# First sequence's scores from unsplit float32 queries and keys, the second's from two parts each

## The chip, the cores and the metric

The kernel runs on one core of one Trainium2 chip. A core has TensorE (PE; its weight loads are listed apart as PEld), VectorE (DVE), ScalarE (ACT), GpSimd (POOL) and SyncE (SP), which each work through a queue of instructions in order and wait for each other by semaphores, and DMA engines that move data between the chip's memory and the on-chip SBUF. TensorE writes to PSUM, eight banks of 512 float32 columns. The metric is the device time of one execution in microseconds, the median of several runs.

## The reference

Three layers follow each other: attention with a sliding window of 128 and 4 sink tokens, a gated MLP, and a layer of 8 experts of which each token takes at most one.

```python
def _attn_ref(q, k, v, n_sink, window):          # q, k, v: (2, 8, 768, 64)
    scores = scale * np.matmul(q, k.transpose(0, 1, 3, 2))
    ...
    scores = np.where(is_sink | in_window, scores, -1000000000.0)
    a = softmax(scores)
    return np.matmul(a, v)

x = attn_out as 1536 tokens of 512
x = (silu(x @ w_gate) * (x @ w_val)) @ w_out     # 512 -> 1536 -> 512
# experts: tokens with x @ w_skip > 0 add gate * relu(x @ w1[e]) @ w2[e], e = argmax(x @ w_gate)
```

## The kernel before, in words

The 1536 tokens are twelve tiles of 128: tiles 0 to 5 are the first sequence, 6 to 11 the second. Attention goes through 48 steps j, one for each tile n and each of four pairs of heads. Step A (step_a) transposes a tile's queries and keys of one pair on TensorE into a PSUM bank (tqk), ScalarE copies the bank to SBUF as the type F32R (fp32r in the rows), a rounded float32, and VectorE subtracts that from the bank, so that a second tile holds what the rounding left. These are kq0x and kq1x for pair x, the first and the second part; each has the keys of the current and of the last tile, four sink keys and the queries. At a sequence's first tile GpSimd copies the sink keys to their place. Step B (step_b) makes the scores of both heads (s0, s1) with three products each: first part by first part, and first by second both ways; the heads lie in partitions 0 to 63 and 64 to 127 of the tiles. VectorE adds the mask and reduces (line 282), ScalarE takes exponentials, VectorE and ScalarE scale the probabilities p. Step D transposes p, and step E multiplies with the values (vb, float32) and writes a tile of the MLP's input, xt, again in two parts.

PSUM is divided by use: two banks "acc", two "acq", two "gv", and two "att". Scores take acc for tiles 0 and 1, acq for tiles 2 and 3, and from tile 4 on att, where the transposes tqk, tpt, tsk and the product with the values (xps) also live. A bank is given out again when its last reader is done, and tqk has two readers, ScalarE's copy and VectorE's subtraction.

The MLP runs in six phases over groups of tiles and 12 chunks of 128 hidden columns. Its weights arrive as pairs of 32-bit words and are converted (lines 135 to 138: two steps on ScalarE, two on VectorE), then split into two parts in a ring of buffers (ScalarE copies, GpSimd or VectorE subtracts). ScalarE's tanh (line 491) evacuates the gate's product of a chunk, in all 52 times. While attention makes the first two tiles, each of its steps adds two small matmuls (warm) that keep TensorE at work. The main program writes attention steps between MLP steps by a fixed quota; a scheduler then sets the order of each engine's queue. From the second MLP phase on, attention of later tiles fills in between MLP matmuls; at the end come the experts.

The helpers that the rows name by line: 69 is act_copy (ScalarE), 72 is lo_of (the subtraction).

## Time and profile before

| | |
|---|---|
| runs | 648.02, 646.52, 643.59 us; median 646.52 |
| profiled execution | 643.09 us, its span from first to last instruction 641.4 us |
| TensorE busy | 593.4 us, 93% of the span |
| VectorE busy | 459.6 us, 72% |
| ScalarE busy | 397.2 us, 62% |
| GpSimd busy | 197.7 us, 31% |
| mean granted TensorE clock | 0.969 of 2.4 GHz |

The profile shows one execution. Busy shares of the whole span are averages over an attention and weight stage, an MLP stage and an expert stage, which have different limits, so views by stretch say more. Ends of matmuls are modelled; their starts are the surer number.

### The profile page before, as it was taken

To read this page: it belongs to the slowest core of one execution; us is meant where nothing else is said; L and a number is where in the kernel's file an instruction comes from. 1 tells how busy PE (TensorE), PEld (TensorE's weight loads), DVE (VectorE), ACT (ScalarE), POOL (GpSimd) and SP (SyncE) were. 2 spreads that over 40 slices of the span, in tenths; PEclk is the share of its full clock that TensorE was granted. 3 is DMA by queue.
4 is the path that set the end of the run, shared out by engine and by line. 5 is a ranking of instruction groups with operands and counts; after the bars stand their busy time and mean duration, and the time that the engine had idled before them with its cause. 6 is when DMAs were issued, how large, how long until landed. Compare 5 with 4: busy or idle time off the path is not lost. (4 is left out here: it accounts for less than half of the span.)

```text
span 641.4 us, 10897 instructions
## 1 busy us (share of the span) xinstructions
PE 593.4 (93%) x3489; PEld 478.6 (75%) x3489; DVE 459.6 (72%) x1163; ACT 397.2 (62%) x892; POOL 197.7 (31%) x289
## 2 busy tenths in 40 slices
PE   4979889889999999999999999999998999999993
PEld 2657667757677787777778899989986777777762
DVE  5789888787656557665665467768848698879961
ACT  4899998899555436554554456657535774856730
POOL 4355657263423022110202030011105353537411
PEclk8798999797999999999999999999999999999998
DMA  8576775464301030200001500003205876977901
GB/s 205 135 196 181 199 204 176 145 193 132 65 2 35 16 106 11 50 1 18 1 1 35 211 30 1 1 35 109 66 34 158 301 264 204 332 232 261 340 4 38
DMA packets 78422, 75.84 MB, mean 118 GB/s; under 512 B 43138, under 2 KB 55426, under 8 KB 78352
## 3 DMA queue, kind: packets, MB, share of 16 engines
q1 hardware_dynamic: 75840, 69.32, 35.2%
q0 software_dynamic: 2512, 5.68, 2.6%
q8 instruction: 32, 0.52, 0.3%
q14 instruction: 38, 0.31, 0.1%
HBM read 65.37 MB, written 11.98 MB: 121 GB/s over the span
## 5 line engine op out<-in xcount | busy, mean ns | idle before, releaser
L454 PE MATMUL gv<-xt,ring 128*128 128x256 f32 (+1 forms) x1248 | 234.4, 336 | 4.2 <-ACT xt L69 2.6
L454 PEld LDWEIGHTS gv<-xt,ring 128*128 128x128 f32 x1248 | 186.0, 192 | 28.6 <-ACT xt L69 3.1
L69 ACT ACTIVATE ring<-w 128x512 fp32r<-128x512 f32 x156 | 98.1, 630 | 96.0 <-PE gv L454 75.0
L72 DVE TENSOR_TENSOR ring<-w,ring 128x512 fp32r<-128x512 f32 x116 | 80.0, 691 | 47.4 <-ACT ring L69 46.8
L466 PE MATMUL acc<-ring,hh 128*128 128x512 f32 x288 | 93.7, 406 | 0.0
L72 DVE TENSOR_TENSOR w<-stage,w 128x512 fp32r<-128x512 f32 x96 | 87.7, 945 | 6.9 <-ACT w L69 4.5
L69 ACT ACTIVATE w<-stage 128x512 fp32r<-128x512 f32 x128 | 73.1, 626 | 10.6 <-DMA stage<-in_moe_w_dram 7.6
L72 POOL TENSOR_TENSOR ring<-w,ring 128x512 fp32r<-128x512 f32 x40 | 53.1, 1331 | 58.8 <-ACT ring L69 53.8
L72 POOL TENSOR_TENSOR w<-stage,w 128x512 fp32r<-128x512 f32 x32 | 46.9, 1468 | 46.8 <-ACT w L69 20.9
L316 POOL TENSOR_SCALAR_AFFINE_SELECT pt<-pt 128x256 f32<-128x256 f32 x40 | 21.0, 525 | 128.9 <-ACT pt L69 128.9
L466 PEld LDWEIGHTS acc<-ring,hh 128*128 128x128 f32 x288 | 51.3, 190 | 10.7 <-ACT hh L69 0.6
L466 PE MATMUL acc<-ring,hl 128*128 128x512 f32 x144 | 58.6, 408 | 0.0
L285 ACT ACTIVATE p<-p,st 128x132 f32<-128x132 f32 x96 | 38.2, 400 | 26.2 <-DVE st L282 26.0
L135 ACT ACTIVATE st<-st 128x512 uint16<-128x512 uint16 x36 | 49.0, 1360 | 3.9 <-DMA st<-in_moe_w_gate_dram 3.3
L869 PE MATMUL yps<-w,hT 128*128 128x512 f32 x192 | 47.1, 399 | 1.0 <-DVE w L72 0.6
L843 PE MATMUL hps<-w,xh 128*128 128x512 f32 x128 | 42.5, 412 | 0.7 <-PEq L917 0.4
L869 PEld LDWEIGHTS yps<-w,hT 128*128 128x128 f32 x192 | 35.3, 188 | 10.4 <-ACTq L917 1.0
L495 DVE TENSOR_TENSOR th<-th,gv 128x256 f32<-128x256 f32 (+1 forms) x52 | 27.1, 521 | 18.5 <-PE gv L454 16.7
L272 PE MATMUL s<-kq 64*128 64x260 f32 (+1 forms) x96 | 27.5, 388 | 11.7 <-DVE st L282 3.2
L640 POOL DMA_INDIRECT xs<-x,pi x12 | 13.3, 1104 | 81.2 <-ACT ring L69 48.6
L272 PEld LDWEIGHTS s<-kq 64*128 64x128 f32 x96 | 13.9, 192 | 31.0 <-issue 14.0
L69 ACT ACTIVATE hh<-th 128x256 fp32r<-128x256 f32 (+1 forms) x52 | 26.2, 503 | 16.6 <-DVE th L495 16.2
(171 smaller groups left out, 989.0 us busy)
## 6 DMA issues: line engine op xcount, KB each, us to landing
stage<-in_moe_w_dram SPq DMA_DIRECT2D x128, 256.0 KB, 4.5
st<-in_moe_w_gate_dram SPq DMA_DIRECT2D x12, 512.0 KB, 4.4
st<-in_moe_w_val_dram SPq DMA_DIRECT2D x12, 512.0 KB, 3.9
st<-in_moe_w_out_dram SPq DMA_DIRECT2D x12, 512.0 KB, 4.6
xs<-trash SPq DMA_DIRECT2D x8, 387.0 KB, 4.8
qk<-in_k_dram SPq DMA_DIRECT2D x12, 256.0 KB, 3.2
qk<-in_q_dram SPq DMA_DIRECT2D x12, 256.0 KB, 4.0
vb<-in_v_dram SPq DMA_DIRECT2D x12, 256.0 KB, 2.8
```

The costliest lines, as they stand in the source:

```text
L69: nc.scalar.activation(out=out, in_=in_, func=ACTF.Copy, scale=scale)
L72: (eng or nc.vector).tensor_tensor(out=out, in0=in_, in1=hi.bitcast(F32), op=ALU.subtract)
L135: nc.scalar.activation(out=h16[x + (0,)], in_=h16[x + (1,)], func=ACTF.Copy, scale=2.0 ** -13, bias=2.0 ** -14 - 0.5)
L272: m_ = nc.tensor.matmul(out=ss[h][:, 0:nk], lhsT=kq[a, pr][r, KW:PW], rhs=kq[c, pr][r, 0:nk], start=m == 0, stop=m == 2)
L285: nc.scalar.activation(out=p[:, h], in_=p[:, h], func=ACTF.Exp, scale=-1.0, bias=st[:, h:h + 1], accum_out=st[:, 2 + h:3 + h])
L316: nc.gpsimd.affine_select(out=d[:, 0], in_=d[:, 1], compare_op=ALU.is_ge, fill=0.0, base=0, pattern=[[0, 2], [1, P]], channel_multiplier=-1)
L454: nc.tensor.matmul(out=ps, lhsT=w_[:, kk * P:(kk + 1) * P], rhs=x_[:, kk, t0 * P:t1 * P], start=kk == 0 and m == 0, stop=kk == KD - 1 and ...
L466: nc.tensor.matmul(out=acc[g, t], lhsT=h_[:, s], rhs=w_, start=c == 0 and m == 0, stop=c == NFC - 1 and m == 2)
L495: nc.vector.tensor_tensor(out=th, in0=th, in1=vp, op=ALU.mult)
L640: d = nc.gpsimd.indirect_dma_start(out=xs[:, :], out_offset=bass.IndirectOffsetOnAxis(ap=pi[:, t], axis=0), in_=x2s[t], in_offset=None, bo ...
L843: nc.tensor.matmul(out=ps[half], lhsT=x_[:, kk, :], rhs=w_[:, kk, :], start=kk == 0 and m == 0, stop=kk == KD - 1 and m == 2)
L869: nc.tensor.matmul(out=y, lhsT=h_[:, c, :], rhs=w_[:, c % 4, :], start=c == 0 and m == 0, stop=c == NF2 - 1 and m == 2)
```

## The change

For tiles 0 to 5 the second parts are not made. Step A copies queries and keys to one float32 tile for each pair, and step B multiplies these as float32, one product for each head in place of three. For tiles 6 to 11 the code does what it did, with new tiles under the same tags.

```diff
--- before.py
+++ after.py
@@ -218,7 +218,12 @@
         return rest
 
 
-    kq = {(hl, pr): att.tile([P, PW], F32R, name=f"kq{hl}{pr}") for hl in range(2) for pr in range(NPAIR)}
+    kq = {}
+
+    def new_kq(pr, parts):
+        for hl in range(len(parts)):
+            kq[hl, pr] = att.tile([P, PW], parts[hl], tag=f"kq{hl}{pr}", name=f"kq{hl}{pr}")
+
     vsk = [None] * B
     prob, psk, pt, xt, skt = {}, {}, {}, {}, {}
 
@@ -242,21 +247,30 @@
         a = t[:, o:o + P]
         return bass.AP(a.tensor, a.offset, [a.ap[0], [step, 2], [1, P]])
 
+    def whole(n):
+
+        return n < NBLK
+
     def step_a(j):
 
         n, pr = divmod(j, NPAIR)
         i = n % NBLK
+        if i == 0 and n <= NBLK:
+            new_kq(pr, [F32] if whole(n) else [F32R, F32R])
         t = attp.tile([P, 512], F32, tag="att", name="tqk")
         for a, src in enumerate((kb[n], qb[n])):
             nc.tensor.transpose(out=t[:, a * P:(a + 1) * P], in_=src[:, 2 * pr:2 * pr + 2, :].rearrange("p h d -> p (h d)"), identity=ident)
         o = (i % 2) * W
         src = t[:, 0:2 * P].rearrange("p (a f) -> p a f", a=2)
-        hi, lo = (two(kq[hl, pr], o, KW - o) for hl in range(2))
-        act_copy(hi, src)
-        lo_of(lo, src, hi)
+        if whole(n):
+            act_copy(two(kq[0, pr], o, KW - o), src)
+        else:
+            hi, lo = (two(kq[hl, pr], o, KW - o) for hl in range(2))
+            act_copy(hi, src)
+            lo_of(lo, src, hi)
         if i == 0:
-            for hl in range(2):
-                nc.gpsimd.tensor_copy(kq[hl, pr][:, P:W], kq[hl, pr].bitcast(F32)[:, 0:4])
+            for hl in range(1 if whole(n) else 2):
+                nc.gpsimd.tensor_copy(kq[hl, pr][:, P:W], (kq[hl, pr] if whole(n) else kq[hl, pr].bitcast(F32))[:, 0:4])
 
     def step_b(j):
 
@@ -266,10 +280,12 @@
         odd = i % 2
         pool, tag = (accp, "acc") if n < GB else (acqp, "acq") if n < GS else (attp, "att")
         ss = [pool.tile([P, 512], F32, tag=tag, name=f"s{h}") for h in range(2)]
-        for m, (a, c) in enumerate(((0, 0), (0, 1), (1, 0))):
+        terms = ((0, 0),) if whole(n) else ((0, 0), (0, 1), (1, 0))
+        for m, (a, c) in enumerate(terms):
             for h in range(2):
                 r = slice(64 * h, 64 * h + 64)
-                m_ = nc.tensor.matmul(out=ss[h][:, 0:nk], lhsT=kq[a, pr][r, KW:PW], rhs=kq[c, pr][r, 0:nk], start=m == 0, stop=m == 2)
+                x_, y_ = kq[a, pr][r, KW:PW], kq[c, pr][r, 0:nk]
+                m_ = nc.tensor.matmul(out=ss[h][:, 0:nk], lhsT=x_, rhs=y_, start=m == 0, stop=m == len(terms) - 1)
         pe_last[:] = [m_.ins]
         if i:
```

The scheduler gives each engine a new order up to the end of the first sequence; behind it the queues are the same but for neighbours that change places. In the new file the lines from 250 on are numbered higher: 272 is 288, 282 is 298, 285 is 301, 454 is 470.

VectorE at the start, before: tmp, kt and mask are pieces of the masks, st and w are weights in conversion, kq_121 and kq_122 the second parts of the first two pairs.

```order
L72 TENSOR_TENSOR kq_121<-tqk,kq_117 128x2x128
L72 TENSOR_TENSOR kq_122<-tqk,kq_118 128x2x128
L137 TENSOR_SCALAR st<-st 128x512
L196 TENSOR_SCALAR mask_110<-kt 128x4
L213 TENSOR_TENSOR tmp<-tmp 128x128
L138 SCALAR_TENSOR_TENSOR w_96<-w_96,st 128x4x128
L196 TENSOR_SCALAR mask_110<-tmp 128x128
L137 TENSOR_SCALAR st<-st 128x512
L550 COPY seen<-first 128x9
L282 ISA p,st<-s_211,mask_109 128x132
```

The same place in the changed kernel:

```order
L196 TENSOR_SCALAR mask_110<-kt 128x4
L566 COPY seen<-first 128x9
L213 TENSOR_TENSOR tmp<-tmp 128x128
L196 TENSOR_SCALAR mask_110<-tmp 128x128
L137 TENSOR_SCALAR st<-st 128x512
L138 SCALAR_TENSOR_TENSOR w_96<-w_96,st 128x4x128
L298 ISA p,st<-s_201,mask_109 128x132
```

The two subtractions are gone, and the second weight's line 137 stands behind the first score reduction (line 298) instead of ahead of it.

ScalarE at the start, before, from its first exponential on; kq_117 and so on are the first parts, pt the transposed probabilities, st a weight in conversion.

```order
L285 ACTIVATE p,st<-p,st 128x132 x2
L69 ACTIVATE kq_119<-tqk 128x2x128
L69 ACTIVATE p<-p,st 128x132
L69 ACTIVATE kq_120<-tqk 128x2x128
L69 ACTIVATE kq_117<-tqk 128x256
L285 ACTIVATE p,st<-p,st 128x132 x2
L69 ACTIVATE pt<-tpt 128x256
L135 ACTIVATE st<-st 128x512
L69 ACTIVATE p<-p,st 128x132
```

The same place in the changed kernel:

```order
L301 ACTIVATE p,st<-p,st 128x132 x2
L69 ACTIVATE kq_220<-tqk 128x2x128
L301 ACTIVATE p,st<-p,st 128x132 x2
L69 ACTIVATE p<-p,st 128x132
L69 ACTIVATE kq_252<-tqk 128x2x128
L301 ACTIVATE p,st<-p,st 128x132
L69 ACTIVATE p<-p,st 128x132
L69 ACTIVATE pt<-tpt 128x256
L301 ACTIVATE p,st<-p,st 128x132
L69 ACTIVATE pt<-tpt 128x256
L69 ACTIVATE kq_158<-tqk 128x256
L69 ACTIVATE p<-p,st 128x132
```

The third weight's line 135 no longer stands among the attention steps of the first tiles; it follows as row 27 where it was row 16.

TensorE at tile 5, pair 1, before: gv is a gate or value product of the MLP, s0 and s1 the scores of the two heads.

```order
L454 MATMUL gv_1575<-xt1_483,ring_106 128x256
L454 MATMUL gv_1575<-xt0_482,ring_106 128x256
L272 MATMUL s0_1590<-kq01_118 128x260
L272 MATMUL s1_1591<-kq01_118 128x260
L272 MATMUL s0_1590<-kq11_122,kq01_118 128x260
L272 MATMUL s1_1591<-kq11_122,kq01_118 128x260
L272 MATMUL s0_1590<-kq01_118,kq11_122 128x260
L272 MATMUL s1_1591<-kq01_118,kq11_122 128x260
L454 MATMUL gv_1611<-xt0_482,ring_106 128x256
```

The same place in the changed kernel:

```order
L470 MATMUL gv_1460<-xt1_444,ring_106 128x256
L470 MATMUL gv_1460<-xt0_443,ring_106 128x256
L288 MATMUL s0_1475<-kq01_164 128x260
L288 MATMUL s1_1476<-kq01_164 128x260
L470 MATMUL gv_1492<-xt0_443,ring_106 128x256
```

Six score matmuls between the same MLP products have become two, which read one tile only.

## Rows read from the trace of the kernel before

**Rows 1.** Busy time by stretch: PE, PEld, DVE, ACT, POOL, granted clock, DMA share, GB/s.
```profile
0.00:30.00 30.00, 21.11 (x110) 14.28 (x112) 18.74 (x99) 19.10 (x52) 10.04 (x38) 0.77 0.69 177
30.00:106.00 76.00, 64.57 (x488) 50.96 (x484) 67.37 (x217) 70.27 (x175) 46.94 (x59) 0.98 0.69 196
106.00:165.00 59.00, 51.72 (x283) 40.55 (x282) 49.92 (x116) 51.87 (x104) 28.73 (x38) 0.88 0.49 148
165.00:480.00 315.00, 314.12 (x1940) 262.98 (x1940) 201.93 (x551) 164.80 (x388) 46.54 (x100) 1.00 0.13 40
```

**Rows 2.** ScalarE's groups up to 106 us: busy us, mean ns, idle before and releaser.
```profile
L135 ACT ACTIVATE st<-st 128x512 uint16<-128x512 uint16 x20 | 27.2, 1359 | 3.3 <-DMA st<-in_moe_w_gate_dram 3.3
L285 ACT ACTIVATE p<-p,st 128x132 f32<-128x132 f32 x40 | 15.7, 397 | 1.6 <-DVE st L282 1.5
L69 ACT ACTIVATE ring<-w 128x512 fp32r<-128x512 f32 x23 | 14.5, 629 | 1.8 <-PE gv L454 1.7
L136 ACT ACTIVATE w<-st 128x512 f32<-128x512 f32 x20 | 13.7, 684 | 0.0
L69 ACT ACTIVATE kq<-tqk 128x256 fp32r<-128x256 f32 x22 | 8.4, 382 | 3.6 <-PE tqk L251 3.5
L69 ACT ACTIVATE p<-p,st 128x132 f32<-128x132 f32 x20 | 8.0, 398 | 1.6 <-DVE st L287 1.4
```

**Rows 3.** Timeline of ScalarE at the first and the seventh tanh: start, us.
```profile
52.16 0.38 ACT L491 ACTIVATE th<-gv 128x256 f32<-128x256 f32 x1 [1.07 <-PE gv L454]
...
106.02 0.39 ACT L491 ACTIVATE th<-gv 128x256 f32<-128x256 f32 x1
```

**Rows 4.** TensorE's waits from 30 to 165 us: total us, times, longest.
```profile
PE tpt L309 <- DVE st L282: 3.2, 3, 1.8
PE s L272 <- DVE kq L72: 2.8, 2, 2.5
```

**Rows 5.** Tile kq up to 139 us: duration ns min/median/max, first and last start.
```profile
L272 PE MATMUL s<-kq,kq x96: 274/280/584, 11.4 to 137.6; 64*128 64x260 f32 x80, 64*128 64x132 f32 x16
...
L69 ACT ACTIVATE kq<-tqk x25: 360/378/487, 5.5 to 135.2; 128x256 fp32r<-128x256 f32 x25
L72 DVE TENSOR_TENSOR kq<-tqk,kq x25: 402/415/454, 10.6 to 136.8; 128x256 fp32r<-128x256 f32 x25
```

**Rows 6.** Timeline of TensorE: one tile's products with values, then one pair's scores.
```profile
65.21 1.97 PE L353 MATMUL xps<-pt,vb 128*64 128x128 f32 x32
...
186.47 0.39 PE L272 MATMUL s<-kq 64*128 64x260 f32 x2
186.70 0.41 PE L272 MATMUL s<-kq,kq 64*128 64x260 f32 x4
187.03 0.73 PE L454 MATMUL gv<-xt,ring 128*128 128x512 f32 x2
```

**Rows 7.** Timeline of all engines at the first scores.
```profile
10.64 0.74 DVE L72 TENSOR_TENSOR kq<-tqk,kq 128x256 fp32r<-128x256 f32 x2
...
10.82 0.33 PE L272 MATMUL s<-kq 64*128 64x132 f32 x2 [2.76 <-POOL kq L259]
...
12.89 0.73 DVE L137 TENSOR_SCALAR st<-st 128x512 uint16<-128x512 uint16 x1
...
13.51 0.28 DVE L282 CUSTOM_DVE_ANT_0 p<-s,mask 128x132 f32<-128x132 f32 x1
```

**Rows 8.** Timeline of all engines at tile 5, pair 1.
```profile
111.60 0.38 PE L272 MATMUL s<-kq 64*128 64x260 f32 x1
111.81 0.36 ACT L69 ACTIVATE kq<-tqk 128x256 fp32r<-128x256 f32 x1
...
113.98 0.41 DVE L72 TENSOR_TENSOR kq<-tqk,kq 128x256 fp32r<-128x256 f32 x1
...
114.45 0.58 PE L272 MATMUL s<-kq 64*128 64x260 f32 x1 [2.47 <-DVE kq L72]
```

**Rows 9.** Busy time by stretch, as rows 1, behind that wait.
```profile
112.00:120.00 8.00, 5.55 (x31) 5.21 (x33) 6.37 (x17) 6.47 (x15) 4.26 (x4) 0.63 0.34 119
```

## Prediction

> **What bounds the kernel now.** I first read the busy time of each engine by stretch [rows 1]. From 165 to 480 us TensorE is busy 314.12 of 315 us at the full granted clock: there the kernel is bound by TensorE, and the second sequence's attention runs inside that stretch. The change touches the first sequence, whose last scores start at 137.6 us [rows 5]. So I read the stretches before 165 us on their own. From 30 to 106 us ScalarE is busy 70.27 of 76 us, VectorE 67.37, TensorE 64.57; from 106 to 165 us 51.87, 49.92 and 51.72 of 59. ScalarE is the fullest engine, but all three are near full and wait for each other. What the front of the kernel gains is carried to the end, because TensorE works without a gap behind it.
>
> Then I read what ScalarE does there [rows 2]: conversions of the weights (1359 + 684 ns each), splits of the weights into the rings (629 ns), and attention in pieces of about 0.4 us. None of this is removed by the change. So the ceiling for a gain is ScalarE's idle time: 10.9 us up to 30 us (19.10 of 30 busy, much of it waiting for the first transposes, 3.5 us, and the first weight, 3.3 us [rows 2]), 5.7 us from 30 to 106, 7.1 us from 106 to 165 [rows 1]. Two landmarks on ScalarE serve as clocks below: the first tanh of the first MLP stage at 52.16 us and the seventh at 106.02 us [rows 3].
>
> Last I read TensorE's waits from 30 to 165 us [rows 4]: 2.8 us in two waits of the scores for the subtraction that makes the second part of queries and keys (line 72 on VectorE), 3.2 us of the probabilities' transposes for VectorE's score reduction. Most of TensorE's idle time is VectorE being late.
>
> **The change part by part.** *VectorE.* In the first sequence 24 subtractions go, 415 ns at the median [rows 5]; 22 of them stand ahead of the seventh tanh, 22 x 0.415 = 9.1 us. VectorE does not set the end by itself, so this is no gain until it shortens a wait of the others.
>
> *ScalarE.* The copy of queries and keys (378 ns [rows 5]) stays and writes float32 in place of the rounded type; the row's own reads of float32 and writes are of the same size, so I take the same time. Counting ScalarE's rows up to the seventh tanh, both programs have 188, the same number of each kind. Its work up to 106.02 us is therefore unchanged, and only its idle time can shrink.
>
> *GpSimd.* Four copies of four columns go, nothing to the sum but at the start (below).
>
> *TensorE.* Per pair of heads six matmuls in three rounds become two float32 matmuls. The scores of this kernel before show no float32 run; the nearest rows are the products with the values, which are float32: 16 written matmuls appear as 32 instructions in 1.97 us [rows 6], so each is two instructions, and a round of two heads takes at most 1.97 / 16 = 123 ns for 128 columns. A pair's scores before: 186.47 to 187.03 us = 0.56 us, the first round 0.23 and the other two 0.33 [rows 6]. With two rounds: if a round grows with its columns, 123 x 260 / 128 = 250 ns, it is 0.25 + 0.25 plus the 0.09 by which the last round before the next full-width matmul exceeds a middle one (0.33 less twice 0.12), 0.59 us. If the round is paced by the weight load and not by columns, it is 0.23 + 0.21 = 0.44 us. The cost is between -0.12 and +0.03 us a pair, -2.9 to +0.7 us over 24 pairs. I take 0, near the upper end, since the value products are the only float32 row and may as well be paced by columns; TensorE has idle time before 165 us to cover either.
>
> The Trainium skill, page "FP8 and Floating Point Precision", section "TensorE Precision Notes", says that true float32 takes four passes through the array. It speaks against the change: four passes for three single ones would be a third more, 0.56 / 3 = 0.19 us a pair by it, +4.5 us over 24 pairs, an estimate from that page and the row; were all of it on the path, the sum would be -0.2 us and the median 646.3. The trace agrees on the passes (two instructions, a round 123 ns for 128 columns, about twice the 53 ns that 128 columns take at 2.4 GHz) but not on the price, since the three rounds before spend 0.23 us on the first one anyway. The sum stands without this.
>
> *The order.* The scheduler moves the start. On VectorE both subtractions and the second weight's bit work leave the place ahead of the first score reduction (line 282, 298 in the new file), which ran at 13.51 us: 0.74 us from 10.64 and 0.73 us from 12.89 [rows 7], which overlap their neighbours a little. The first scores themselves waited 2.76 us until 10.82 us for GpSimd's copy behind the subtraction [rows 7]; they need only ScalarE's copy now, but the reduction needs its mask, which VectorE makes first. Start: **-1.2 us**, bounds 0 and -2.8.
>
> ScalarE does attention first and pushes the third weight back, from its 16th row to its 27th. Up to the first tanh it has 8 conversions in place of 10, 4 ring splits in place of 6, but one more each of exponential, scaling and transposed copy: 2 x 2.04 + 2 x 0.63 - 3 x 0.4 = 4.1 us less [rows 2]. This is no gain: the 4.1 us come back before the seventh tanh. The first tanh must come by 48.1 us for ScalarE to be even. VectorE's queue up to there is shorter as well, by 11 subtractions, 4.6 us, and two weights' bit work, so I expect it to be even.
>
> *30 to 106 us.* Most of the 22 subtractions lie here. Up to the seventh tanh ScalarE waits for VectorE 1.5 us (reduction) and 1.4 us (reciprocal) [rows 2]. I take somewhat under half of these 2.9 us: **-1.2 us**; bounds +4.1 (the push-back is not made up) and -5.7 (all idle time).
>
> *106 to 165 us.* At 111.60 us TensorE starts the scores of tile 5, pair 1; the second head's scores need a PSUM bank of the two that all attention steps share from tile 4 on, and it still holds the next pair's transposes. ScalarE has read them by 111.81 + 0.36 = 112.17 us, VectorE reads them at 113.98 only, and TensorE stands 2.47 us until 114.45 [rows 8]. After the change that bank is free at ScalarE's read: 114.45 - 112.17 = **-2.3 us**. Right behind, in 112 to 120 us, the granted clock is 0.63 of 2.4 GHz [rows 9], part of the time at 1.2 GHz, after the engine had stood still: 0.37 x 8 = 3.0 us of full-rate time. I leave that out of the forecast, as another wait can drop the clock; with it the term is -5.3, with a new wait in its place 0.
>
> *From 165 us* ScalarE's and TensorE's rows stand in the same order but for neighbours, with the second sequence as it was: 0. Where the new tiles replace the first sequence's under the same names, the copy into them waits for the last scores that read the old ones, as it did within one tile before; nothing is queued behind it that was not.
>
> The sum is -1.2 - 1.2 - 2.3 = -4.7 us. The profiled execution took 643.09 us (span 641.4), 3.4 us under the median 646.52, so it would be 638.4, and the median **641.8, say 642 us**, 0.7% less. About 1% is what a measurement of this kernel can tell from no change, as the three runs before lie 4.4 us apart.
>
> **The rivals.** *Both waits and the clock come back.* For it: TensorE stands 18.7 us from 30 to 165 us [rows 1], and most of it is lateness of the engine that loses work. Against it: ScalarE has only 12.9 us to give there. Price: -1.2 - 2.4 - 2.3 - 3.0 = -8.9, 637.6 us at the median.
>
> *ScalarE swallows it.* Its rows up to 106 us are the same 188 and it is busy 92% from 30 us on, so VectorE's 9.1 us turn into idle time of VectorE. Price 0 to -1: 646 us. Against it: the wait at 114.45 us is TensorE's and is certainly gone in that form.
>
> *Slower: the pushed-back conversions are not made up.* At the start ScalarE has weights to convert while attention waits for TensorE, which runs at 1.2 GHz for part of the first 30 us (granted 0.77 [rows 1]). If attention is bound by its own chain there, ScalarE idles with the weights queued behind, the first tanh stays at 52.16 us and ScalarE owes 4.1 us after it. It decides from 48.1 us on: each microsecond that the first tanh comes later than that is one lost. Price +4.1: 650.6 us.
>
> *The heads do not run side by side in float32.* The value products show pairs at the same time in halves of the columns; the scores use halves of the rows, where this case shows only the rounded type. Then a pair takes 0.25 x 4 + 0.09 = 1.09 us, +0.53 a pair, +13 us of TensorE work before 165 us, against 18.7 us idle; if a third of it comes through, +4, it cancels the gain: 646 us.
>
> **How the numbers follow.** Forecast 0.42; both waits and the clock 0.24; swallowed 0.17; slower by owed conversions 0.11; heads one after another 0.06. The range 634.5 to 649 holds the first, the second with 3 us beyond it for the unknown rounds of float32 (-2.9), the third and the last; the fourth is left out with the tails. Faster by over 1% (under 640.1): nearly all of the second and a quarter of the forecast, 0.32. Slower by over 1% (over 653): a half of the fourth, 0.06. Within 1%: 0.62.
>
> **What the new profile would show.** VectorE with 24 subtractions into kq in place of 48, about 10 us less busy; scores of 260 columns as 2 instructions a head in rounds near 0.25 us, heads together; the first tanh by 48.1 us, the seventh near 103.5; no wait of the scores of tile 5 for line 72; TensorE full from about 160 us. I would be wrong if the first tanh comes after 50 us, if rounds take 0.5 us, or if the waits on VectorE's reductions grow by what the subtractions gave.

## The result and the profile after

The changed kernel is slower: 655.23 us median against 645.06 us for the kernel before on the same chip, ratio 1.0147 with a 95% interval of 1.0104 to 1.019. Executions that fall into a slower state are left out of a ratio, which is not the plain quotient of the two medians printed beside it and differs from it by up to 0.4% here and below. The prediction was 642 us, 0.7% faster, with a range up to 649 us. The profiled execution after took 653.13 us (span 651.4) against 643.09 us (span 641.4): 10 us more.

Busy time by stretch in the changed kernel, in the stretches of [rows 1]:

```profile
0.00:30.00 30.00, 18.57 (x86) 11.51 (x87) 16.92 (x87) 17.18 (x47) 9.33 (x34) 0.83 0.64 158
30.00:106.00 76.00, 63.31 (x429) 48.20 (x427) 60.67 (x190) 66.82 (x165) 42.47 (x54) 0.91 0.64 177
106.00:165.00 59.00, 51.69 (x297) 39.62 (x296) 47.91 (x122) 53.81 (x112) 27.38 (x39) 0.94 0.57 172
165.00:480.00 315.00, 312.03 (x1898) 259.93 (x1895) 205.10 (x553) 166.62 (x392) 52.09 (x104) 0.99 0.14 40
```

ScalarE (the fourth busy figure) does 17.18 us of work in the first 30 us where it did 19.10, and 66.82 in the next 76 us where it did 70.27. It is the fullest engine there, and it got emptier. Its own clocks, the first, the seventh and the thirteenth tanh, in the timeline of the changed kernel (line 507 is 491 of before, the first two answer to [rows 3]):

```profile
53.70 0.38 ACT L507 ACTIVATE th<-gv 128x256 f32<-128x256 f32 x1 [1.43 <-PE gv L470]
...
113.19 0.38 ACT L507 ACTIVATE th<-gv 128x256 f32<-128x256 f32 x1
...
189.01 0.58 ACT L507 ACTIVATE th<-gv 128x512 f32<-128x512 f32 x1
```

Before they stood at 52.16, 106.02 and 180.06 us. So 1.5 us are lost by the first tanh, another 5.6 by the seventh, another 1.8 by the thirteenth, 8.95 together; from there to the end of the span it is 462.4 us in place of 461.3. These steps mix work that moved with waiting, so here is the busy time between the same landmarks, in the kernel before:

```profile
0.00:52.16 52.16, 38.61 (x240) 27.08 (x241) 38.94 (x160) 39.93 (x100) 22.21 (x52) 0.84 0.70 182
52.16:106.02 53.86, 47.09 (x354) 38.18 (x352) 47.19 (x155) 49.46 (x127) 34.79 (x46) 1.00 0.67 198
106.02:180.06 74.04, 66.31 (x357) 51.63 (x355) 57.38 (x140) 59.08 (x125) 32.62 (x44) 0.91 0.42 125
```

and in the changed kernel:

```profile
0.00:53.70 53.70, 37.03 (x223) 24.70 (x224) 35.44 (x151) 37.05 (x99) 19.79 (x48) 0.86 0.62 158
53.70:113.19 59.49, 51.90 (x335) 40.65 (x335) 46.52 (x142) 52.81 (x128) 36.51 (x48) 0.92 0.65 189
113.19:189.01 75.82, 66.07 (x344) 49.79 (x342) 56.95 (x137) 59.08 (x124) 32.23 (x41) 0.91 0.45 127
```

ScalarE's idle time, the stretch less its busy time, grows by 4.4 us ahead of the first tanh (12.2 to 16.6), by 2.3 to the seventh and by 1.8 to the thirteenth. Most of the 5.6 us between the first and the seventh tanh is work that was pushed there: 52.81 us in place of 49.46. The thirteenth tanh is the landmark from here on. Busy time up to it, in the kernel before:

```profile
0.00:180.10 180.10, 152.05 (x946) 116.90 (x946) 143.51 (x453) 148.50 (x350) 89.61 (x140) 0.91 0.58 163
```

and in the changed kernel:

```profile
0.00:189.00 189.00, 154.99 (x898) 115.14 (x898) 138.91 (x429) 148.92 (x349) 88.53 (x136) 0.90 0.56 155
```

ScalarE works 148.5 and 148.9 us up to there: the same work. It stands idle 31.6 us before and 40.1 us after. Nearly all of the loss ahead of the thirteenth tanh, 8.5 of 8.95 us, is idle time of ScalarE. Up to there it waits for VectorE's steps on the scores, the reduction and the reciprocal (total us, times, longest), in the kernel before:

```profile
ACT p L285 <- DVE st L282: 5.4, 8, 1.7
ACT p L69 <- DVE st L287: 3.4, 8, 0.7
```

and in the changed kernel:

```profile
ACT p L301 <- DVE st L298: 11.5, 13, 3.0
ACT p L69 <- DVE st L303: 6.6, 12, 1.7
```

Together that is 8.8 us before and 18.1 after: the growth of 9.3 us accounts for the added idle time, while ScalarE's waits for TensorE stay about as they were (17.0 and 15.9 us). VectorE, with 24 subtractions fewer up to there, is late more often. A wait is put down to what ended it; what kept VectorE is another question. One of these waits, in the timeline of all engines of the changed kernel:

```profile
82.62 0.39 ACT L301 ACTIVATE p<-p,st 128x132 f32<-128x132 f32 x1
82.72 0.73 DVE L137 TENSOR_SCALAR st<-st 128x512 uint16<-128x512 uint16 x1
82.91 0.19 ACT L301 ACTIVATION_READ_ACCUMULATOR p<-p,st 128x1 f32 x1
...
83.56 0.84 DVE L138 SCALAR_TENSOR_TENSOR w<-w,st 128x512 int32<-128x512 int32 x1
...
84.32 0.37 DVE L302 TENSOR_SCALAR st<-st 128x2 f32<-128x2 f32 x1
...
84.72 0.17 DVE L303 RECIPROCAL st<-st 128x2 f32<-128x2 f32 x1
...
84.98 0.41 ACT L69 ACTIVATE p<-p,st 128x132 f32<-128x132 f32 x1 [1.20 <-DVE st L303]
```

ScalarE's second exponential of a pair is done at about 83.1 us with its sum. The next VectorE steps of that chain are two operations on two columns (lines 302 and 303). In VectorE's queue the bit work of a weight (lines 137 and 138, 1.6 us) stands ahead of them, and ScalarE, which needs the reciprocal, waits until 84.98 us. TensorE's waits from 30 to 165 us, as [rows 4]:

```profile
PE tpt L325 <- DVE st L298: 6.0, 3, 2.5
PE gv L470 <- ACT xt L69: 5.3, 2, 3.2
PE s L288 <- DVE st L298: 1.5, 2, 1.2
```

The wait for line 72 at tile 5 [rows 8] is gone. Another, as long, is new:

```profile
116.78 0.41 PE L325 MATMUL tpt<-ident,p 128*128 128x128 f32 x2 [2.47 <-DVE st L298]
```

### The profile page after: what moved, and what is told of

Same layout as the page of the kernel before. It is cut to its first block, busy times and chain, and to the rows that moved or that the text cites. A ratio compares the mean times of both kernels' runs of the same rounds, so it can differ in the third digit from the quotient of the medians.

```text
span 651.4 us, 10770 instructions
## 1 busy us (share of the span) xinstructions
PE 597.1 (92%) x3441; PEld 477.5 (73%) x3441; DVE 455.3 (70%) x1139; ACT 397.9 (61%) x892; POOL 196.9 (30%) x285
## 5 line engine op out<-in xcount | busy, mean ns | idle before, releaser
L470 PE MATMUL gv<-xt,ring 128*128 128x256 f32 (+1 forms) x1248 | 238.4, 340 | 5.9 <-ACT xt L69 5.3
L470 PEld LDWEIGHTS gv<-xt,ring 128*128 128x128 f32 x1248 | 189.4, 196 | 33.8 <-ACT xt L69 5.9
L72 POOL TENSOR_TENSOR ring<-w,ring 128x512 fp32r<-128x512 f32 x40 | 53.3, 1339 | 53.4 <-ACT ring L69 47.5
L482 PEld LDWEIGHTS acc<-ring,hh 128*128 128x128 f32 x288 | 51.5, 191 | 11.0 <-issue 0.9
L288 PE MATMUL s<-kq 64*128 64x260 f32 (+1 forms) x144 | 36.4, 418 | 9.1 <-POOL kq L273 2.8
L885 PEld LDWEIGHTS yps<-w,hT 128*128 128x128 f32 x192 | 35.3, 188 | 10.4 <-ACTq L933 1.0
L137 DVE TENSOR_SCALAR st<-st 128x512 uint16<-128x512 uint16 x36 | 29.9, 832 | 12.7 <-ACT st L135 12.6
L288 PEld LDWEIGHTS s<-kq 64*128 64x128 f32 x144 | 17.7, 197 | 28.0 <-issue 14.1
```

The lines of the kernel that those rows point to most:

```text
L72: (eng or nc.vector).tensor_tensor(out=out, in0=in_, in1=hi.bitcast(F32), op=ALU.subtract)
L137: nc.vector.tensor_scalar(out=h16[x + (1,)], in0=h16[x + (3,)], scalar1=0x8000, scalar2=None, op0=ALU.bitwise_and)
L288: m_ = nc.tensor.matmul(out=ss[h][:, 0:nk], lhsT=x_, rhs=y_, start=m == 0, stop=m == len(terms) - 1)
L470: nc.tensor.matmul(out=ps, lhsT=w_[:, kk * P:(kk + 1) * P], rhs=x_[:, kk, t0 * P:t1 * P], start=kk == 0 and m == 0, stop=kk == KD - 1 and ...
L482: nc.tensor.matmul(out=acc[g, t], lhsT=h_[:, s], rhs=w_, start=c == 0 and m == 0, stop=c == NFC - 1 and m == 2)
L885: nc.tensor.matmul(out=y, lhsT=h_[:, c, :], rhs=w_[:, c % 4, :], start=c == 0 and m == 0, stop=c == NF2 - 1 and m == 2)
```

## The experiments

Each run is compared with the kernel before on the same chip. The table has all of them; up to the thirteenth tanh, "busy" is ScalarE's busy time, "idle" is the tanh's start less that, and "for VectorE" is the sum of its waits for VectorE's steps on the scores, all of the profiled execution.

| kernel | ratio (95%) | 1st tanh | 1st to 7th | 13th tanh | busy | idle | for VectorE | 13th to end |
|---|---|---|---|---|---|---|---|---|
| before | 1 | 52.2 | 53.9 | 180.1 | 148.5 | 31.6 | 8.8 | 461.3 |
| changed | 1.0147 (1.0104 to 1.019) | 53.7 | 59.5 | 189.0 | 148.9 | 40.1 | 18.1 | 462.4 |
| run 1 | 1.0024 (0.9989 to 1.0059) | 54.3 | 54.0 | 182.1 | 148.4 | 33.7 | 10.1 | 465.1 |
| run 2 | 1.0033 (0.9999 to 1.0068) | 54.6 | 59.3 | 184.8 | 149.7 | 35.1 | 10.4 | 462.0 |
| run 3 | 1.0007 (0.9981 to 1.0034) | 51.5 | 56.1 | 184.9 | 150.1 | 34.8 | 8.6 | 461.8 |
| run 4 | 1.015 (1.008 to 1.0219) | 58.1 | 59.6 | 191.5 | 149.0 | 42.5 | 16.8 | 462.1 |
| run 5 | 1.0073 (1.0038 to 1.0108) | 54.5 | 58.2 | 186.3 | 149.3 | 37.0 | 15.1 | 462.2 |
| run 6 | 1.0114 (1.0046 to 1.0181) | 57.5 | 61.0 | 191.4 | 149.4 | 42.0 | 14.4 | 462.6 |
| run 7 | 1.0025 (0.9995 to 1.0055) | 56.0 | 54.1 | 186.5 | 149.1 | 37.4 | 9.4 | 463.1 |
| run 8 | 1.0065 (1.0033 to 1.0097) | 59.3 | 56.5 | 186.6 | 149.0 | 37.6 | 11.8 | 462.5 |
| run 9 | 0.9959 (0.9923 to 0.9995) | 54.6 | 53.8 | 181.1 | 147.3 | 33.8 | 10.1 | 462.2 |
| run 10 | 0.996 (0.9927 to 0.9993) | 54.4 | 53.6 | 180.1 | 147.7 | 32.4 | 8.7 | 461.6 |
| run 11 | 0.9917 (0.9882 to 0.9952) | 51.0 | 53.3 | 177.9 | 147.1 | 30.8 | 9.3 | 461.4 |
| run 12 | 1.0263 (1.0192 to 1.0334) | 65.8 | 60.8 | 200.7 | 149.0 | 51.7 | 24.3 | 461.3 |
| run 13 | 1.014 (1.007 to 1.021) | 51.9 | 64.4 | 189.1 | 148.6 | 40.5 | 14.5 | 462.3 |
| run 14 | 1.0053 (1.0024 to 1.0082) | 55.6 | 57.2 | 188.1 | 148.7 | 39.4 | 11.9 | 461.4 |
| run 15 | 1.0133 (1.0051 to 1.0216) | 57.1 | 57.4 | 186.6 | 148.5 | 38.1 | 14.2 | 460.8 |

Two columns are nearly constant: ScalarE's work (147 to 150 us) and, but for run 1, the time behind the thirteenth tanh (461 to 463 us). The kernels differ by ScalarE's idle time in front. Its waits for VectorE sort them: 8.6 to 10.4 us in the kernel before and in the seven runs with a ratio up to 1.0033, 11.8 us and more in the eight runs above 1.005 and in the changed kernel. TensorE's granted clock up to the thirteenth tanh does not sort them: it is 0.91 before, 0.90 in the changed kernel and 0.95 in run 9, but also 0.95 in run 4, which loses 1.5%. Single executions scatter (run 15's profiled one took 649.2 us, its median is 653.0), and the one of the kernel before, 643.09 us, was among its fastest, 2 to 5 us under the medians that the runs are compared with. So the ratio decides, the columns say where, and a difference of one or two us in them says little.

The first theories were Q, that the conversions pushed back in ScalarE's queue cost it, and F, that the float32 products do.

### Run 1: the sequences change places

```diff
-        return n < NBLK
+        return n >= NBLK
```

> The two sequences change places: tiles 0 to 5 are split in two parts as in the kernel before, tiles 6 to 11 go through unsplit float32. Up to the first sequence's end ScalarE's queue has the weight conversions where the kernel before has them (10 ahead of the first tanh). Theory Q (queue): the loss of the changed kernel comes from the conversions that ScalarE's queue puts behind the attention steps; here there is none of that, so the time is that of the kernel before plus what TensorE, which is full there, pays for the products: a pair of 0.64 us in place of 0.56, 24 x 0.08 = +1.9 us, ratio 1.000 to 1.005. Theory F (float32): the products themselves cost the 9.5 us, by their own time and by what waits behind them; then it is slower here too, where TensorE is full and every one counts, ratio 1.008 or more.

Measured 648.99 against 646.99 us, 1.0024. A pair at full clock, in the timeline of TensorE of this run, to be held against [rows 6]:

```profile
197.49 0.71 PE L288 MATMUL s<-kq 64*128 64x260 f32 x4
198.13 0.72 PE L482 MATMUL acc<-ring,hh 128*128 128x512 f32 x2
```

From the pair's start to the next matmul it is 0.64 us, 0.56 before. The time behind the thirteenth tanh grows by 3.8 us in this one execution; the medians give 2.0 us, and 24 x 0.08 is 1.9. So F is worth about 2 us where TensorE is full; the interval ends at 1.0059, 3.8 us, and leaves no room for the 9.5 us of theory F.

### Run 2: conversions earlier

```diff
+    def early_w(n):
+        p = tc.cur_priority
+        tc.cur_priority = p - n
+        convert_w()
+        tc.cur_priority = p
...
-            convert_w()
+            early_w(60)
```

> The changed kernel, with the weight conversions that the start loop issues given an earlier place in the scheduler's priority: the third conversion stands at row 20 of ScalarE's queue in place of 30, and 9 conversions are ahead of the first tanh in place of 8. The arithmetic is the changed kernel's. Theory Q: most of the loss goes, ratio to the kernel before 0.995 to 1.005, and the first tanh comes by 53 us with one conversion more behind it. Theory F: the loss stays, ratio 1.012 or more.

In the trace the third conversion is ScalarE's row 18 before and row 30 in the changed kernel, where the prediction counted 16 and 27.

Measured 648.34 against 646.99 us, 1.0033: with the change's arithmetic untouched, most of the loss goes. So far for Q, but the edit gives every queue a new order, and ScalarE still needs 59.3 us from the first to the seventh tanh; it makes up behind the seventh.

### Run 3: one rounded part, one product

```diff
-            new_kq(pr, [F32] if whole(n) else [F32R, F32R])
+            new_kq(pr, [F32R] if whole(n) else [F32R, F32R])
...
-                nc.gpsimd.tensor_copy(kq[hl, pr][:, P:W], (kq[hl, pr] if whole(n) else kq[hl, pr].bitcast(F32))[:, 0:4])
+                nc.gpsimd.tensor_copy(kq[hl, pr][:, P:W], kq[hl, pr].bitcast(F32)[:, 0:4])
```

> The changed kernel, with the first sequence's queries and keys in one part of the rounded type in place of float32: one single-pass product a head. It leaves out the contribution of the second parts to the first sequence's scores. The queues are the changed kernel's (third conversion at row 31, 8 ahead of the first tanh), TensorE's time for a pair of scores is about 0.25 us in place of 0.64. Theory Q: slow as the changed kernel, ratio to the kernel before 1.008 to 1.018. Theory F: the loss goes and turns into a gain, ratio 0.985 to 1.000.

Measured 646.70 against 646.99 us, 1.0007: neither theory. The conversions stand where the changed kernel has them and the loss is gone, against Q; 7.4 us of TensorE's work are gone too and nothing is gained, against F. The order as a whole is not the changed kernel's: up to the thirteenth tanh, 239 of ScalarE's 293 instructions and 291 of VectorE's 367 follow each other as there.

### Run 4: the kernel before with conversions later

The function early_w is that of run 2, here and in runs 6 to 8.

```diff
-            convert_w()
+            early_w(-400)
```

> The kernel before, its arithmetic untouched, with the conversions that the start loop issues given a later place: the fourth conversion stands at row 44 of ScalarE's queue in place of 29, and 9 are ahead of the first tanh in place of 10. Theory Q: slower than the kernel before by half of the loss or more, ratio 1.005 to 1.015. Theory F: as the kernel before, ratio 0.997 to 1.003.

Measured 655.63 against 646.99 us, 1.015: an edit of the order alone costs as much as the change, at the top of what Q had said.

### Run 5: three products of the one part, no subtraction

```diff
-        terms = ((0, 0),) if whole(n) else ((0, 0), (0, 1), (1, 0))
+        terms = ((0, 0),) * 3 if whole(n) else ((0, 0), (0, 1), (1, 0))
...
```

It stands on run 3's edit, and each of the three products starts anew.

> The changed kernel, with the first sequence's queries and keys in one part of the rounded type, multiplied three times over (each product starts anew, so the second parts' contribution is left out): TensorE's time for a pair is that of the kernel before, 0.56 us, VectorE's 24 subtractions are gone as in the change, and the scheduler leaves the conversions where the kernel before has them (rows 18, 29, 45 of ScalarE's queue, 10 ahead of the first tanh). What is left is VectorE's relief alone. The prediction's sum for it was -4.7 us, ratio 0.993. Theory M, as the first four runs leave it: the loss is the queue's (some 7 us) and the products' own price (some 2 us), and the relief is worth little: ratio 0.993 to 1.000. Were the relief itself harmful (earlier steps of attention that crowd ScalarE), it would be 1.005 or more.

Measured 651.42 against 646.25 us, 1.0073. TensorE's work is that of the kernel before, VectorE has less, the conversions stand nearly where they stood, and it is slower. Q, even mixed with F (theory M), falls here: the conversions' place does not decide alone.

### Run 6: conversions earlier still

```diff
-            convert_w()
+            early_w(110)
```

> The changed kernel with the start loop's conversions moved forward further: rows 20, 24, 29, 37 of ScalarE's queue, 11 ahead of the first tanh in place of 8 (and 9 in the second run). Theory M: what is left of the loss after the second run (1.0033) is the price of the float32 products, which no order gives back: ratio 0.999 to 1.006. If it were only the order, the ratio goes on falling with the conversions ahead, to 0.990 to 0.998; if conversions too far forward hold attention back, it is 1.006 or more.

Measured 655.29 against 646.25 us, 1.0114: three conversions more than the changed kernel ahead of the first tanh, and most of the loss is back, the third of the outcomes named. The first tanh comes at 57.5 us.

### Run 7: run 3 with conversions earlier

```diff
-            convert_w()
+            early_w(60)
```

> The third run's kernel (one part, one product, the second parts' contribution left out) with the third to sixth conversion at rows 20, 28, 37, 47 of ScalarE's queue in place of 31, 38, 47, 56; 8 ahead of the first tanh as there. Theory M: the place of these four conversions is worth here what it was with float32, 1.0147 to 1.0033, so 1.0007 falls to 0.988 to 0.995. If short products had hidden the queue's cost, it stays at 0.998 to 1.003.

Measured 647.65 against 646.25 us, 1.0025; run 3 was 1.0007. What had brought 1.1% in run 2 brings nothing here: a miss for M.

### Run 8: the kernel before with conversions earlier

```diff
-            convert_w()
+            early_w(60)
```

> The kernel before, arithmetic untouched, with the start loop's conversions moved forward: the fifth at row 34 of ScalarE's queue in place of 47, the sixth at 42 in place of 53, 11 ahead of the first tanh in place of 10. Theory M: if conversions at the start only fill ScalarE's idle time, it gains up to what one conversion costs, 2 us, ratio 0.995 to 1.001. If the place in the kernel before is already the right one, 1.001 to 1.006.

Measured 651.11 against 646.25 us, 1.0065. Later costs (run 4), and so does earlier. That leaves theory O: the order of all queues together is what the kernel before has, and every new one that the scheduler made was the same or worse. The next runs tie the order itself.

### Run 9: the change in the old order

At the end of attention and MLP, the rows of each queue up to the end of the first sequence are tied one behind the other, without a semaphore. The numbers are places in the program as it is written out, listed in the order in which the kernel before issues them.

```diff
+QUEUES = {
+    "PE": [
...
+    def pin():
+        for engine, rows in QUEUES.items():
...
+            for a, b in zip(rows, rows[1:]):
+                tc.add_manual_dep(traced[b], traced[a].name, mybir.DependencyInfo(mybir.DependencyClass.NoSync, mybir.DependencyReason.DATA), reason="queue")
...
+    pin()
     count_tokens(attp)
```

> The changed kernel, all of its arithmetic as it is, with the queues of TensorE, VectorE, ScalarE, GpSimd and SyncE tied row by row to the order of the kernel before up to the end of the first sequence (the rows that the change removes are simply absent). Theory O (order): the loss comes from the order that the scheduler makes anew, and the change itself is worth -4.7 us (the prediction's sum for VectorE's relief) to 0, plus 24 x 0.08 = 1.9 us at most for the products: ratio 0.993 to 1.003. Theory A (arithmetic): unsplit float32 costs as such, 1.010 or more.

Measured 644.27 against 647.99 us, 0.9959: the same instructions as the changed kernel, 1.9% faster than it and 0.4% faster than the kernel before, this last by an interval that ends at 0.9995, just under no change. Busy time up to its thirteenth tanh:

```profile
0.00:181.10 181.10, 154.62 (x898) 112.40 (x898) 134.20 (x429) 147.32 (x349) 88.94 (x136) 0.95 0.58 162
```

The counts are those of the changed kernel (898 matmuls, 429 of VectorE, 349 of ScalarE); VectorE's busy time is 9.3 us under that of before, close to the 24 x 0.415 = 10 us of the subtractions, and ScalarE waits for it little more than before. Its waits for VectorE's steps on the scores up to the thirteenth tanh (lines 366 and 371 are 298 and 303 of the changed kernel):

```profile
ACT p L369 <- DVE st L366: 6.5, 7, 3.2
ACT p L137 <- DVE st L371: 3.6, 9, 0.7
```

10.1 us, where the changed kernel has 18.1 and the kernel before 8.8. In the trace the queues of VectorE, GpSimd and TensorE up to there, leaving aside what works on kq, are row for row those of the kernel before, and so is ScalarE's whole queue. The kernel before tied to its own order was not run; that tying rows does not help by itself is seen from runs 12, 13 and 15, which are tied and slow. This is the version that beats both kernels.

### Run 10: run 5 in the old order

```diff
+    pin()
     count_tokens(attp)
```

The tables of run 9, with three matmuls a head in TensorE's, on run 5's kernel.

> The fifth run's kernel (three products of the one rounded part, each starting anew, no subtraction; the second parts' contribution to the first sequence's scores is left out) with all five queues tied to the order of the kernel before. TensorE's work for the scores is that of the kernel before, so this is VectorE's relief alone in an unchanged order. If the prediction's terms hold, -4.7 us, ratio 0.993; if VectorE's time there is slack, 0.998 to 1.002. Against the fifth run (1.0073), which had the order of its own scheduler, it tells what that order costs: 1.005 or more here would mean that the relief itself hurts.

Measured 643.42 against 647.99 us, 0.996. Run 5 has the same arithmetic and 1.0073: the order alone is 1.1%. It lies between the two outcomes named. Against run 9, float32 and three rounded products differ in front by less than these runs can tell.

### Run 11: run 3 in the old order

```diff
+    pin()
     count_tokens(attp)
```

The tables of run 9 on run 3's kernel.

> The third run's kernel (one part, one product a head, the second parts' contribution to the first sequence's scores left out) with all five queues tied to the order of the kernel before. TensorE has 24 x 0.31 = 7.4 us less to do than the kernel before. Theory O: what the order took away in the third run (1.0007) comes out as a gain: 0.982 to 0.994. If TensorE's time before 165 us is slack, it is as the tenth run.

Measured 641.52 against 647.99 us, 0.9917; run 3 was 1.0007. The gain that run 3 lacked had gone into its order. Against run 10, 7.4 us less work of TensorE bring 1.9 us at the medians, so TensorE's time in front is slack for the most part, not all.

### Run 12: the kernel before in the new order

```diff
+    pin()
     count_tokens(attp)
```

The tables, here of ScalarE, VectorE and GpSimd, list the rows as the changed kernel issues them.

> The kernel before, all of its arithmetic as it is, with the queues of ScalarE, VectorE and GpSimd tied to the order of the changed kernel up to the end of the first sequence; its 24 subtractions and TensorE's queue are left to the scheduler. Theory O: slower than the kernel before by most of the loss, 1.008 to 1.020. Theory A: as the kernel before, 0.997 to 1.004.

Measured 663.63 against 647.99 us, 1.0263: slower than the change itself and above what theory O had said, though the arithmetic is that of before. It is not the plain reverse of run 9. TensorE's queue was left free and came out as a third order: up to the thirteenth tanh 705 of 772 matmuls other than scores follow each other as in the kernel before and 699 as in the changed kernel, while those two share 724; and the subtractions went where the scheduler put them. So it shows that an order can cost as much as 2.6%, not that the changed kernel's own order costs all of that. Up to its thirteenth tanh:

```profile
0.00:200.70 200.70, 165.41 (x946) 124.15 (x946) 146.21 (x453) 149.02 (x349) 88.40 (x140) 0.86 0.52 146
```

### Run 13: the old order up to the first tanh

The pieces shown here and in runs 14 and 15 are against run 9.

```diff
-        203, 204, 205, 194, 195, 206, 207, 214, 215, 216, 217, 218, 219, 220, 212, 213, 208, 209, 210, 211, 221, 222, 223, 224, 225, 229, 230, 231, 232, 233,
...
+        203, 204, 205, 194, 195, 206, 207, 214, 215, 216, 217, 218, 219, 220, 212, 213, 208
```

The tables of run 9, each cut at the first tanh (the piece shown is the end of TensorE's).

> The changed kernel with all five queues tied to the order of the kernel before up to the first tanh only (79 rows of ScalarE, 218 matmuls); behind it the scheduler orders anew. If the loss is what ScalarE's queue owes at the first tanh (two conversions and two ring splits, as the prediction's slower rival had it), most of it goes: ratio 0.995 to 1.004. If the order behind the first tanh carries as much, 1.006 to 1.012.

Measured 654.95 against 646.90 us, 1.014. The first tanh is back at 51.9 us and the loss is as large: the order that the scheduler makes anew behind it, which is not the changed kernel's either, costs as much. Busy time of this run from 30 us to the first tanh, then to the seventh:

```profile
30.00:51.90 21.90, 17.55 (x130) 12.16 (x127) 17.93 (x59) 20.89 (x49) 12.21 (x14) 0.96 0.69 185
51.90:116.40 64.50, 54.91 (x339) 42.52 (x337) 46.20 (x145) 52.06 (x129) 34.39 (x49) 0.88 0.61 176
```

ScalarE is idle 12.4 of the 64.5 us, against 4.4 of 53.9 before. One wait there, in the timeline of all engines:

```profile
78.70 0.61 ACT L100 ACTIVATE ring<-w 128x512 fp32r<-128x512 f32 x1
78.91 0.69 DVE L169 SCALAR_TENSOR_TENSOR w<-w,st 128x512 int32<-128x512 int32 x1
...
79.40 1.33 POOL L103 TENSOR_TENSOR ring<-w,ring 128x512 fp32r<-128x512 f32 x1 [1.19 <-ACT ring L100]
79.52 1.24 DVE L333 TENSOR_SCALAR st<-st 128x2 f32<-128x2 f32 x1
...
80.87 0.15 DVE L334 RECIPROCAL st<-st 128x2 f32<-128x2 f32 x1
...
81.40 0.41 ACT L100 ACTIVATE p<-p,st 128x132 f32<-128x132 f32 x1 [2.08 <-DVE p L339]
```

It is the pattern of the changed kernel once more: bit work ahead of the two small operations, then a small operation that takes 1.24 us while GpSimd's split of a ring, begun 0.12 us earlier, runs to its end, and ScalarE idle for 2.08 us. The kernel before has such a place too (its line 286 takes 1.19 us at 63.21 us, between the same bit work), so these rows are examples and not the difference.

### Run 14: ScalarE's queue alone in the old order

```diff
-    "PE": [
...
-    "DVE": [
...
-    "Pool": [
...
-    "SP": [
...
```

> The changed kernel with ScalarE's queue alone tied to the order of the kernel before up to the end of the first sequence; the other queues are ordered around it by the scheduler. If ScalarE's order is the cause, ratio 0.993 to 1.003, as with all queues tied. If TensorE's and VectorE's own order carries it, 1.006 or more.

Measured 650.21 against 646.90 us, 1.0053, between the two outcomes named: about two thirds of the loss against the kernel before goes, half of the way to run 9.

### Run 15: every queue but ScalarE's in the old order

```diff
-    "Activation": [
...
```

> The changed kernel with the queues of TensorE, VectorE, GpSimd and SyncE tied to the order of the kernel before, ScalarE's left to the scheduler, which puts 169 of its 615 rows elsewhere. If ScalarE's order is the cause, 1.006 or more; if the others' order carries it, 0.993 to 1.003.

Measured 653.03 against 646.90 us, 1.0133, above 1.006 as forecast if ScalarE's order is the cause. Four executions from 649 to 659 us leave it open how much of the loss goes; the interval begins at 1.0051, above all of run 9's. So neither part of the old order is enough alone: ScalarE's rows must stand right, and the other engines' rows around them. How the loss divides between them these two runs do not tell, as their intervals overlap.

## Why the prediction was wrong

**The step that failed** is the order. The prediction counted ScalarE's rows up to the seventh tanh, found 188 in both programs, and concluded that its work there is unchanged "and only its idle time can shrink", and it took VectorE, with a shorter queue, to come no later. ScalarE's work is unchanged (148.5 and 148.9 us up to the thirteenth tanh), but its idle time grew by 8.5 us, because in the new order it waits 18.1 us for VectorE's reductions and reciprocals where it waited 8.8. A queue in order can have the same rows and wait longer between them. The same instructions in the old order (run 9) wait 10.1 us and come to 0.9959, not 1.0147; the two other arithmetics gain from the old order as well, 1.0073 to 0.996 (runs 5 and 10) and 1.0007 to 0.9917 (runs 3 and 11).

Of the three signs that it named for being wrong, two came. The first tanh stands at 53.7 us, after 50; and the waits on VectorE's reductions, with the reciprocals, grew by 9.3 us, about the 9.1 us that the subtractions gave, though no run shows that the two sizes are linked. The rounds are 0.32 us, not 0.5.

**The slower rival** was the nearest, and its chance of 0.11 too low. It had ScalarE idle at the start, with 4.1 us of work owed behind the first tanh. That much came: 4.4 of the 8.5 us of added idle time lie ahead of the first tanh, which is late (53.7 us, not 48.1), and behind it ScalarE has 3.4 us more to do up to the seventh. What it had wrong is whom ScalarE waits for and where the loss ends. It put the idle time down to attention behind a slow TensorE, but the granted clock of the first 30 us rose from 0.77 to 0.83, and the waits that grew ahead of the first tanh are those for VectorE's steps on the scores, 1.1 to 5.1 us (for TensorE 6.5 to 7.7). And it stopped at the start, while 4.1 us more of idle time follow behind the first tanh. The place of the first tanh says little by itself: four kernels in one and the same order (before, runs 9, 10 and 11) have it anywhere from 51.0 to 54.6 us, and run 13 has it at 51.9 us and loses as much.

**The terms, in an unchanged order.** Run 9 measures them together: 0.9959 of 646.52 us is 643.9 us, -2.6 where the sum was -4.7; the interval runs from -5.0 to -0.3 and just holds the sum. The terms one by one rest on single executions, in which run 9's (645.09 us) is slower than the one of the kernel before (643.09), so one or two us in them are not settled:

*106 to 165 us, -2.3:* the wait went as forecast, the gain was smaller. In runs 9, 10 and 11 the stretch from the seventh to the thirteenth tanh takes 72.7, 72.1 and 73.5 us, 74.0 before: -1.3, -1.9 and -0.5. TensorE no longer waits for line 72 at tile 5, and the granted clock, 0.63 in [rows 9], is 1.00 from 112 to 120 us of run 9:

```profile
112.00:120.00 8.00, 7.06 (x66) 5.96 (x66) 7.64 (x20) 7.29 (x18) 4.99 (x5) 1.00 0.31 97
```

Run 9 has other waits of TensorE for VectorE instead, one of 2.66 us at 165.03 us where the kernel before has 1.43. In the changed kernel a wait for VectorE's reduction, also 2.47 us, stands there, and the clock is 0.85.

*30 to 106 us, -1.2:* nothing is to be seen. From the first to the seventh tanh run 9 takes 53.8 us, 53.9 before. VectorE's 9.1 us turned into idle time of VectorE, as the rival "ScalarE swallows it" had it.

*Start, -1.2:* not to be seen either. The first scores of the changed kernel wait for GpSimd's copy as before, and start at 11.12 us, not earlier than the 10.82 of [rows 7]:

```profile
10.54 0.20 POOL L211 COPY mask<-mask 128x4 f32<-128x4 f32 x1 [5.63 <-DVE code L561]
10.76 0.10 POOL L564 MEMSET first<- 128x1 f32 x1
10.80 0.42 POOL L273 COPY kq<-kq 128x4 f32<-128x4 f32 x2
```

The copy stands in GpSimd's queue behind a mask that waits 5.63 us for VectorE's constants, and that wait was there before too; the prediction had put the copy's lateness down to the subtraction. The first reduction came at 13.13 us, 0.4 us earlier, and no tanh shows it.

*TensorE, 0 with +0.03 us a pair as the upper bound:* too low. A pair takes 0.64 us, +0.08, in two rounds of 0.32 us. The prediction took 0.25 for a round, scaled from the value products by columns; what the other 0.07 us of a round is no run isolates. The heads do run side by side, and that rival is out. In front the price is not to be told from none (0.9959 and 0.996 in runs 9 and 10); where TensorE is full, run 1's 1.0024 fits it, though its interval holds no change as well. Four passes for three, the estimate from the Trainium skill, page "FP8 and Floating Point Precision", section "TensorE Precision Notes", gave 0.56 + 0.19 = 0.75 us a pair; the trace has 0.64.

*From 165 us, 0:* right. From the thirteenth tanh on it is 461 to 463 us in all but run 1.

**What stays open.** The runs show that the order is the cause, that neither ScalarE's old queue nor the other old queues are enough alone, and that a loss can sit ahead of the first tanh (most of run 12's) or behind it (run 13's). The waits show where it goes, to ScalarE waiting for VectorE's steps on the scores. They do not name single rows: which rows of VectorE's queue stand in the way in all these waits was not counted, and the two waits shown are examples. Why the scheduler finds another order for so small an edit was not looked into. TensorE's queue of the changed kernel on the arithmetic of before was not tried.

## What to carry to other kernels

Where a scheduler orders the queues, an edit is two changes: its arithmetic and a new order, and in a stretch where three engines are 85% to 92% busy the order weighs more (here -0.4% and +1.9%). Tie the rows to the old order, or tie the old arithmetic to the new order, before calling an edit fast or slow. Equal rows up to a landmark promise equal work, not equal waiting: sum up what the fullest engine waits for, before and after, and look in the new order for long independent operations that now stand between two short steps of a dependent chain, and give such a forecast a wide range on the slow side.

## What the runs showed of the hardware

A float32 matmul of two heads in halves of the rows appears as two instructions a head, here with the duration that the changed kernel's rows give, single heads included:

```profile
L288 PE MATMUL s<-kq x92: 273/424/799, 11.1 to 135.9; 64*128 64x260 f32 x76, 64*128 64x132 f32 x16
L69 ACT ACTIVATE kq<-tqk x24: 362/384/406, 5.8 to 135.2; 128x256 f32<-128x256 f32 x24
```

ScalarE's copy costs the same in float32 as in the rounded type (384 and 378 ns [rows 5]).

VectorE's operation on 128x2 elements takes 0.17 us at the median and 1.24 us in the row at 79.52 us of run 13. It ended at 80.76 us, 0.03 us after GpSimd's operation of 79.40 to 80.73. The Trainium skill, page "SBUF — State Buffer", section "SBUF: two separate sides", says that the two engines share a pair of ports as an exclusive lock, which the one that starts first keeps for its whole instruction, where VectorE's operation is in a mode that uses both ports or has two inputs in SBUF. The row agrees, though no run shows which mode this operation ran in, and it shows that so small an operation can pay the full length of the other. The wait at tile 5 in the kernel before [rows 8] looks the same: just ahead of line 72 VectorE's lines 292 and 295 took 1.24 and 1.26 us, where their medians are 0.29 and 0.17, and each ended within 0.1 us of one of GpSimd's ring splits.
